# First attention on TensorE: global queries of two pairs in column strips, local probabilities as weights, the result turned back

## The chip, the cores and the metric

The kernel runs on one core of a Trainium2 chip. The metric is device time in microseconds. Before the change three runs took 511.86 to 514.08 us, with a median of 514.04 us. The engines are TensorE (PE, with its weight loads as PEld), VectorE (DVE), ScalarE (ACT), GpSimd (POOL) and SyncE (SP), whose queue issues all DMAs.

## What is computed

Three stages for 4 batches. The first attention has 8 heads of 64, 512 local tokens and 32 global ones. Global queries look at all keys, local queries at the global keys and at a window of 32 to either side. The second stage routes the 576 tokens over 4 experts by a gate (each expert is one causal attention head), and the third is an MLP with a convolution of three taps and a gate.

```python
k_all = np.concatenate([k_g, k_l], axis=2)
out_g = sm(scale * q_g @ k_all.T) @ v_all
mask = np.abs(pos[:, None] - pos[None, :]) <= window
out_l = sm(concat(scale * q_l @ k_g.T, where(mask, scale * q_l @ k_l.T, -1e9))) @ concat(v_g, v_l)
...
a = sm(where(causal, -1e9, scale * q @ k.T))
out += mask * w * (a @ v @ wo[e])
...
h = np.maximum(x @ w_in, 0.0)
gate = 1.0 / (1.0 + np.exp(-conv_out))
return h * gate @ w_out
```

## The kernel before

Every operation is first recorded as a node with a due time (`due`) and an estimated cost (`cost_pe`, `cost_act`, `cost_dve`, `cost_pool`, `cost_dma`). `Recorder.schedule` (lines 227 to 307) then plays the nodes through in estimated time: each engine takes, of the nodes whose inputs and buffers are free, the one with the earliest due time. The order that comes out is written into each engine's queue; on the chip each engine keeps to it. So due times are priorities and not start times, and since `emit` issues everything (line 314), all rows of the trace have that line and are told apart by tile and shape. Due times come from the constants of lines 37 to 40: `PERIOD` between batches, `A_AT` and `A_STEP` for the first attention, `B_AT`, `LAST`, `ITEMS` and `ITEM_STEP` for the second, `C_AT`, `C_HALF` and `C_PROJ` for the MLP, `FOLD` and `WOUT` with their steps for preparing weights.

Heads go in pairs, with the 64 dims of two heads on 128 partitions; a batch has 4 pairs, the run 16. For a pair, `phase_a` (line 670) does this in turn.

- `load_kq` and `load_v` fetch keys and queries in one DMA (tile `raw`, two buffers) and the values in two (`vr`, three buffers for two halves each). The global queries of the pair's two heads are laid out with zeros, so that one matmul over 128 rows gives both heads' scores.
- `scores_g` (571) makes 64 rows of scores (2 heads of 32 queries) over 544 keys in two matmuls of 480 and 64 columns. VectorE takes the maxima, ScalarE the exponentials into `Pg`, VectorE the sums, and POOL scales `Pg`.
- `scores_l` (587) makes the local scores: 16 groups of 32 queries, each over 128 keys, in tiles of 64 rows by 32 columns, after a mask (`lmask`) has been put into PSUM by bf16 matmuls. VectorE takes the maxima, ScalarE eight exponentials into two tiles `Pa`, and POOL scales both by one over the sums (lines 613 and 614).
- `trans_g` and `trans_l` turn `Pg` and `Pa` by transposes on TensorE; ScalarE copies the results out of PSUM (`PGT`, `PA`).
- `pv_l` (637): the values are the weights (128 x 64) and the turned probabilities move, 32 columns each, 32 matmuls a pair. The result has dims on the partitions, as the next stage wants it.
- `pv_end` (650) splits the result into a high and a low part (`xh` by ScalarE, `xl` by VectorE), then does the global queries' values.

In the trace each fp32 matmul that is no transpose stands as two records.

`phase_b` does the second attention: projections of q, k, v from `xh`, `xl`, the gate, then eight items (score, transpose, values). Its turned probabilities lie in `PT` (two buffers) and `PLT`; its results in `oh` and `ol`. `phase_c` does the MLP from `oh` and `ol`, in two halves of eight column blocks with a projection after each.

Weights of the MLP come as 64-bit words. `decode` (437) makes floats of a chunk of 256 columns: four ops on VectorE, an add on POOL, an absolute value on ScalarE and, on VectorE, a guard that zeroes what is too small (line 450). 16 chunks of `w_in` are folded with `wo` on TensorE (`fold_gen`), 16 chunks of `w_out` only split (`wout_gen`). The fold keeps `wo` in the memory of `oh` and `ol`, so the second attention's first results wait for the fold.

PSUM has five buffers `s` (scores and projections) and three buffers `t` (transposes and values).

Of the kernel before, what the change touches and what calls it, by code (L numbers as in the profile page):

```python
# [21 lines left out]
EPS = 1e-9  # L22
# [362 lines left out]
def body(ctx, tc, kq, vA, w_gate, wqk, wv, woT, w_in, conv_w, w_out, cmask, out):  # L385
# [13 lines left out]
    def due(us):  # L399
        rec.due = us  # L400
# [65 lines left out]
    trif = T([128, 4, 4], F32, "trif")  # L466
    cw = T([128, 3, 8], F32, "cw")
# [79 lines left out]
    NPA, NPT = 2, 2  # L547
# [4 lines left out]
    Pg = T([64, 6, 128], F32, "Pg")  # L552
# [3 lines left out]
    QW = SL + 2 * SG  # L556
# [14 lines left out]
    def scores_g(k, q):  # L571

        mg = T([64, 8], F32, "mg", 2)
        gt = PS(5, 96)[:64], PS(64)[:64]
        for z, kk in enumerate((k[:, 32:672].rearrange("p (m c) -> p m c", m=5)[:, :, 32:], k[:, 672:736])):
            if z == 0:
                rec.claim(Pg)
            pe.matmul(gt[z], q[:, SL:], kk, start=True, stop=True)
            dve.tensor_reduce(mg[:, z:z + 1], gt[z], axis=AX.X if z else AX.XY, op=ALU.max, negate=True)
        dve.tensor_scalar(mg[:, 2:3], mg[:, 0:1], mg[:, 1:2], SCALE, op0=ALU.min, op1=ALU.mult)  # L580
        for z, d in enumerate((Pg[:, 0:5, 32:128], Pg[:, 5, 32:96])):
            act.activation(d, gt[z], AF.Exp, bias=mg[:, 2:3], scale=SCALE, accum_out=mg[:, 4 + z:5 + z])
# [4 lines left out]
    def scores_l(k, q):  # L587
# [16 lines left out]
        ml = T([128, 2, 16], F32, "ml", 2)  # L604
        for y in range(2):
            dve.tensor_reduce(ml[:, y, 0:4], t[y], axis=AX.X, op=ALU.max, negate=True)
            dve.tensor_scalar(ml[:, y, 0:4], ml[:, y, 0:4], SCALE, None, op0=ALU.mult)
            for i in range(4):
                act.activation(P[y][:, i], t[y][:, i], AF.Exp, bias=ml[:, y, i:i + 1], scale=SCALE,
                               accum_out=ml[:, y, 4 + i:5 + i])  # L610
        dve.tensor_scalar(ml[:, :, 8:12], ml[:, :, 4:8], EPS, None, op0=ALU.add)
        dve.reciprocal(ml[:, :, 12:16], ml[:, :, 8:12])
        for y in range(2):
            pool.tensor_tensor(P[y], P[y], ml[:, y, 12:16, None].to_broadcast([128, 4, 128]), op=ALU.mult)
        return P

    def trans_g():
        PGT = T([128, 6, 64], F32, "PGT")
        t = PO(6, 64)
        rec.claim(PGT)  # L620
        with rec.group():
            for m in range(6):
                pe.transpose(t[:, m, :], Pg[:, m], ident[:64, :64])
        act.activation(PGT, t, AF.Copy)
        return PGT

    def trans_l(P):
        PA = T([128, 4, 128], F32, "PA", 2)
# [8 lines left out]
    def pv_l(b, c, vr, PA):  # L637

        o = PO(4, 128)
        xh, xl = xs[b, c] = T([128, S], F32R, "xh", XB), T([128, S], F32R, "xl", XB)  # L640
        rec.claim(xh, xl)
        with rec.group():
            for g in range(NG_):
                q = slice(32 * (g % 4), 32 * (g % 4) + 32)
                for y in range(2):
                    pe.matmul(o[64 * y:64 * y + 64, g // 4, q], vr[g // 8][:, g % 8, 64 * y:64 * y + 64], PA[y][:, g // 4, q],
                              start=True, stop=True)
        return o
# [15 lines left out]
    def consts_a():  # L664
        due(-15)
# [26 lines left out]
    def phase_b(b):  # L692
# [265 lines left out]
def host_layout(inputs):  # L958
# [23 lines left out]
    kq = np.zeros((B, H // 2, 2, D, KB + SL + 2 * SG), kl.dtype)  # L982
# [8 lines left out]
    for y in range(2):  # L991
        kq[:, :, y, :, KB + SL + SG * y:KB + SL + SG * y + SG] = pair(inputs["q_g"])[:, :, y]
# [26 lines left out]
```

## Time and profile before

| | |
|---|---|
| Median of 3 runs | 514.04 us (511.86 to 514.08) |
| Profiled execution, its own time | 516.68 us |
| Its span in the trace | 514.9 us |
| TensorE busy | 468.6 us, 91% |
| TensorE weight loads | 400.2 us, 78% |
| VectorE busy | 359.1 us, 70% |
| ScalarE busy | 313.5 us, 61% |
| POOL busy | 155.5 us, 30% |
| Moved by DMA | 44.06 MB |

The profile shows one execution. Busy time is the time in which an engine had an instruction running; matmuls are pipelined and their records overlap, so a busy TensorE need not be at its peak. A wait is put down to the last thing that an engine waited for. What lies outside the span, some 1.8 us here, belongs to the time but not to the trace.

### The profile page before, as it was taken

To read this page: it belongs to the slowest core of one execution; us is meant where nothing else is said; L and a number is where in the kernel's file an instruction comes from. 1 tells how busy PE (TensorE), PEld (TensorE's weight loads), DVE (VectorE), ACT (ScalarE), POOL (GpSimd) and SP (SyncE) were. 2 spreads that over 40 slices of the span, in tenths; PEclk is the share of its full clock that TensorE was granted. 3 is DMA by queue.
4 is the path that set the end of the run, shared out by engine and by line. 5 is a ranking of instruction groups with operands and counts; after the bars stand their busy time and mean duration, and the time that the engine had idled before them with its cause. 6 is when DMAs were issued, how large, how long until landed. Compare 5 with 4: busy or idle time off the path is not lost.

```text
span 514.9 us, 14575 instructions
## 1 busy us (share of the span) xinstructions
PE 468.6 (91%) x5688; PEld 400.2 (78%) x5688; DVE 359.1 (70%) x1026; ACT 313.5 (61%) x1048; POOL 155.5 (30%) x259
## 2 busy tenths in 40 slices
PE   3559869987989799999999999999999999999997
PEld 1346559964678589997779999877888999787896
DVE  1878876898989987385659763667486564665961
ACT  1666564556579776565569864447696764344972
POOL 2335445445771635022440200225212200322000
PEclk9788898998999889999999999999999999999999
DMA  8484533242055060014044030002421000000011
GB/s 308 165 241 163 181 136 104 87 135 95 26 176 178 25 217 22 22 35 127 23 137 134 27 105 1 11 23 68 137 83 66 24 0 3 23 23 1 1 45 45
DMA packets 19045, 44.06 MB, mean 86 GB/s; under 512 B 2848, under 2 KB 8096, under 8 KB 18976
## 3 DMA queue, kind: packets, MB, share of 16 engines
q1 hardware_dynamic: 18976, 43.12, 25.2%
q8 instruction: 45, 0.74, 0.6%
q14 instruction: 24, 0.20, 0.1%
HBM read 38.66 MB, written 4.46 MB: 84 GB/s over the span
## 4 chain that ended last, share of the span: by engine, by line
PE 68%; DVE 16%; DMA 6%; ACT 5%; POOL 3%; issue 2%; SPq 0%; POOLq 0%; ACTq 0%; DVEq 0%
PE s L314 52%; PE t L314 16%; DVE cv L314 7%; DMA raw<-in_kq_dram 3%; DMA w<-in_w_in_dram 2%; DVE hb L314 2%; DVE gl L314 1%; DVE mg L314 1%; DVE stB L314 1%; DVE ml L314 1%; POOL w L314 1%; ACT hb L314 1%; POOL Pa L314 1%; ACT Pa L314 1%; DVE wqkl L314 1%
## 5 line engine op out<-in xcount | busy, mean ns | idle before, releaser
L314 PE MATMUL s<-gh,wuh 128*128 128x272 f32 x256 | 78.9, 308 | 0.4 <-ACT gh L314 0.4
L314 DVE SCALAR_TENSOR_TENSOR cv<-hb,cw,cv 128x272 f32<-128x272 f32 x128 | 66.6, 535 | 16.6 <-ACT cv L314 14.8
L314 POOL TENSOR_SCALAR w<-w,stB,gate 128x128 f32<-128x128 f32 (+3 forms) x64 | 41.5, 659 | 116.0 <-DVE gate L314 51.2
L314 PE MATMUL s<-gl,wuh 128*128 128x272 f32 x256 | 74.9, 293 | 1.4 <-DVE gl L314 1.2
L314 PE MATMUL s<-gh,wul 128*128 128x272 f32 x256 | 74.2, 290 | 0.0
L314 PEld LDWEIGHTS s<-gh,wuh 128*128 128x128 f32 x256 | 48.8, 191 | 5.8 <-issue 3.0
L314 POOL TENSOR_TENSOR Pa<-Pa,ml 128x512 f32<-128x512 f32 x32 | 37.3, 1183 | 46.4 <-DVE ml L314 24.8
L314 PEld LDWEIGHTS s<-gl,wuh 128*128 128x128 f32 x256 | 48.8, 191 | 2.8 <-DVE gl L314 2.6
L314 PE MATMUL s<-raw 64*32 64x128 f32 (+2 forms) x1088 | 43.7, 308 | 7.8 <-DMA raw<-in_kq_dram 6.7
L314 PEld LDWEIGHTS s<-gh,wul 128*128 128x128 f32 x256 | 48.7, 190 | 0.0
L314 ACT ACTIVATE Pa<-s,ml 128x128 f32<-128x128 f32 x128 | 45.3, 378 | 3.3 <-DVE ml L314 2.8
L314 ACT ACTIVATE w<-s,stB 128x128 f32<-128x128 f32 (+3 forms) x64 | 33.4, 527 | 18.8 <-DVE stB L314 10.7
L314 PE MATMUL s<-oh,wfh 128*128 128x274 f32 x128 | 39.8, 311 | 1.1 <-ACT Pa L314 1.1
L314 POOL TENSOR_TENSOR cv<-cv,hb 128x256 f32<-128x256 f32 (+1 forms) x33 | 26.0, 788 | 48.8 <-DVE hb L314 39.3
L314 PEld LDWEIGHTS s<-raw 64*32 64x32 f32 (+1 forms) x1088 | 22.9, 117 | 20.7 <-issue 11.1
L314 DVE COPY PT<-t 128x128 f32<-128x128 f32 (+3 forms) x64 | 29.8, 485 | 12.0 <-PE t L314 11.4
L314 PE MATMUL s<-xh,wqkh 128*128 128x272 f32 x128 | 37.6, 294 | 0.1
L314 PE MATMUL s<-xh,wqkl 128*128 128x272 f32 x128 | 37.4, 292 | 0.0
L314 PE MATMUL s<-xl,wqkh 128*128 128x272 f32 x128 | 37.4, 292 | 0.0
L314 PE MATMUL s<-ol,wfh 128*128 128x274 f32 x128 | 37.3, 291 | 0.0
L314 PE MATMUL s<-oh,wfl 128*128 128x274 f32 x128 | 37.2, 291 | 0.0
L314 DVE TENSOR_REDUCE stB<-s 128x1 f32<-128x128 f32 (+3 forms) x64 | 29.7, 484 | 8.6 <-PE s L314 6.1
(147 smaller groups left out, 1302.8 us busy)
## 6 DMA issues: line engine op xcount, KB each, us to landing
vr<-in_vA_dram SPq DMA_DIRECT2D x32, 512.0 KB, 5.1
raw<-in_kq_dram SPq DMA_DIRECT2D x16, 672.0 KB, 4.7
out_dram<-y SPq DMA_DIRECT2D x32, 136.0 KB, 1.7
w<-in_w_in_dram SPq DMA_DIRECT2D x16, 256.0 KB, 3.5
w<-in_w_out_dram SPq DMA_DIRECT2D x16, 256.0 KB, 2.7
w<-in_wqk_dram SPq DMA_DIRECT2D x4, 256.0 KB, 5.4
w<-in_wv_dram SPq DMA_DIRECT2D x4, 128.0 KB, 4.1
w<-in_woT_dram SPq DMA_DIRECT2D x2, 256.0 KB, 2.7
```

The costliest lines, as they stand in the source:

```text
L314: getattr(n.eng.nc, method)(*map(real, args), **{k: real(v) for k, v in kw.items()})
```

## The change

- `scores_g` takes two pairs at once. Each of the four heads is a matmul of 64 rows by 32 columns with its own column strip, so that 128 rows of scores come out; `Pg` has 128 partitions, and the maxima, exponentials, sums and the scaling are done once for two pairs. The zeros in the global queries' layout are gone.
- Keys and queries come in two DMAs with tiles of their own (`rk`, `rq`, two buffers each).
- `scores_l` no longer scales the probabilities. It returns one over the sums.
- `pv_l`: the turned probabilities (128 x 32) are the weights, the values move with 64 columns. The result has queries on the partitions; VectorE multiplies it by one over the sums into `x`, and `pv_end` turns it back with four transposes. The global values are now `pv_g`.
- `PA`, `PT`, `PLT` (its first 128 keys by four) and `x` share four buffers, `p2`.
- The guard in `decode` goes from one op on VectorE to two on POOL.
- An exponential of one column is done first of all, which loads ScalarE's table.
- `lmask` is due ahead of the first pair's loads.
- All constants of the order are new, and two costs of TensorE.

```diff
-PERIOD, A_AT, A_STEP, LOAD_AHEAD = 60.0, -1.0, 10.0, 20.0
-B_AT, LAST, ITEMS, ITEM_STEP = 30.0, 35.0, 13.5, 2.4
-C_AT, C_HALF, C_PROJ = 75.0, 23.0, 11.0
-FOLD, FOLD_STEP, WOUT, WOUT_STEP = 20.5, 2.5, 75.0, 2.5
+PERIOD, A_AT, A_STEP, LOAD_AHEAD = 54.5, 0.0, 5.0, 21.5
+B_AT, LAST, ITEMS, ITEM_STEP = 29.0, 54.0, 9.0, 2.45
+C_AT, C_HALF, C_PROJ = 80.0, 41.0, 36.5
+FOLD, FOLD_STEP, WOUT, WOUT_STEP = 12.0, 1.45, 75.0, 2.0
...
     if K == 64:
-        return us + 0.052
+        return us + max(0.03, N / 2400 if N > 128 else 0.0)
+    if M == 32 and N == 64:
+        return us + 0.03
...
-        dve.scalar_tensor_tensor(dst, a, GUARD, d, op0=ALU.is_ge, op1=ALU.mult)
+        pool.tensor_scalar(a, a, GUARD, 1.0, op0=ALU.is_ge, op1=ALU.mult)
+        pool.tensor_tensor(dst, a, d, op=ALU.mult)
...
+    due(-30)
+    warm = T([128, 1], F32, "warm")
+    dve.memset(warm, 0.0)
+    act.activation(warm, warm, AF.Exp)
...
-        raw = T([128, KB + QW], F32, "raw", 2)
-        sp.dma_start(raw, kq[n // 4, n % 4])
-        return raw[:, :KB], raw[:, KB:]
+        k, q = T([128, KB], F32, "rk", NRK), T([128, QW], F32, "rq", NRQ)
+        sp.dma_start(k, kq[n // 4, n % 4][:, :KB])
+        sp.dma_start(q, kq[n // 4, n % 4][:, KB:])
+        return k, q
...
+        with rec.group():
+            for z in range(2):
+                for c, (k, q) in enumerate(pairs):
+                    for y in range(2):
+                        kk = k[64 * y:64 * y + 64]
+                        kk = kk[:, 672:736] if z else kk[:, 32:672].rearrange("p (m c) -> p m c", m=5)[:, :, 32:]
+                        r = slice(64 * c + 32 * y, 64 * c + 32 * y + 32)
+                        pe.matmul(gt[z][r] if z else gt[z][r].rearrange("p (m c) -> p m c", m=5),
+                                  q[64 * y:64 * y + 64, SL:], kk, start=True, stop=True)
...
-        for y in range(2):
-            pool.tensor_tensor(P[y], P[y], ml[:, y, 12:16, None].to_broadcast([128, 4, 128]), op=ALU.mult)
-        return P
+        return P, ml[:, 3]
...
-                    pe.matmul(o[64 * y:64 * y + 64, g // 4, q], vr[g // 8][:, g % 8, 64 * y:64 * y + 64], PA[y][:, g // 4, q],
-                              start=True, stop=True)
+                    d = slice(64 * y, 64 * y + 64)
+                    pe.matmul(o[r, i, d], PA[y][:, i, r], vr[g // 8][:, g % 8, d], start=True, stop=True)
+        heads = lambda t: t.rearrange("p i (y d) -> p i y d", d=64)
+        dve.tensor_tensor(heads(x), heads(o), one[:, :, :, None].to_broadcast([128, 4, 2, 64]), op=ALU.mult)
+        return x
...
+            for i in range(4):
+                pe.transpose(t[:, i, :], x[:, i], ident)
...
     def consts_a():
-        due(-15)
+        due(-25)
...
     def phase_a(b):
-        for c in range(4):
+        for c in range(0, 4, 2):
+            at = A_AT + PERIOD * b + A_STEP * c
             n = 4 * b + c
-            at = A_AT + PERIOD * b + A_STEP * c
             due(at - LOAD_AHEAD)
-            kq_ = load_kq(n)
-            vr = load_v(n)
+            kq_ = [load_kq(n), load_kq(n + 1)]
+            vr = []
+            for y in range(2):
+                due(at + A_STEP * y - LOAD_AHEAD)
+                vr.append(load_v(n + y))
             due(at)
-            scores_g(*kq_)
-            due(at + 1)
-            P = scores_l(*kq_)
+            scores_g(kq_)
+            P = []
+            for y in range(2):
+                due(at + 1 + A_STEP * y)
+                P.append(scores_l(*kq_[y]))
             due(at + A_STEP)
             PGT = trans_g()
-            PA = [trans_l(P[y]) for y in range(2)]
-            due(at + A_STEP + 1)
-            o = pv_l(b, c, vr, PA)
-            pv_end(b, c, o, vr, PGT)
+            for y in range(2):
+                due(at + A_STEP * (y + 1))
+                PA = [trans_l(p) for p in P[y][0]]
+                due(at + A_STEP * (y + 1) + 1)
+                x = pv_l(vr[y], PA, P[y][1])
+                pv_end(b, c + y, x)
+                pv_g(b, c + y, vr[y], PGT)
...
-                PT = T([128, 4, 128], F32, "PT", NPT)
+                PT = T([128, 4, 128], F32, "p2", NPT)
```

## Rows read from the trace of the kernel before

**Rows 1.** The page: busy us of each engine, share of the span, instructions.
```profile
PE 468.6 (91%) x5688; PEld 400.2 (78%) x5688; DVE 359.1 (70%) x1026; ACT 313.5 (61%) x1048; POOL 155.5 (30%) x259
```

**Rows 2.** Six stages: length, busy us (instructions), clock (1.00 is 2.4 GHz), DMA share, GB/s.
```profile
0.00:15.00 15.00, 6.18 (x85) 3.61 (x86) 3.54 (x11) 2.63 (x6) 3.29 (x11) 1.00 0.86 311
15.00:75.00 60.00, 44.30 (x761) 31.57 (x759) 49.16 (x118) 37.28 (x142) 29.36 (x31) 0.86 0.52 164
75.00:105.00 30.00, 27.90 (x265) 27.10 (x267) 23.10 (x71) 16.31 (x57) 12.82 (x16) 0.94 0.34 116
105.00:180.00 75.00, 63.82 (x920) 48.66 (x916) 70.12 (x201) 51.59 (x179) 40.57 (x58) 0.95 0.32 107
180.00:450.00 270.00, 267.38 (x3191) 236.83 (x3183) 175.42 (x532) 170.25 (x571) 61.62 (x118) 0.99 0.19 62
450.00:515.00 65.00, 59.07 (x489) 52.42 (x487) 37.71 (x96) 35.39 (x98) 7.87 (x26) 1.00 0.07 23
```

**Rows 3.** Waits of TensorE: line waiting, releaser, us in total, times, longest.
```profile
PE s L314 <- DMA raw<-in_kq_dram: 6.7, 4, 4.8
...
PE t L314 <- POOL Pa L314: 5.4, 6, 3.9
...
PE s L314 <- DVE lmask L314: 4.1, 1, 4.1
...
PE s L314 <- DVE wfl L314: 3.1, 1, 3.1
...
PE t L314 <- DVE PT L314: 1.4, 3, 0.8
```

**Rows 4.** Timeline of the start, all engines: start us, length us, what.
```profile
7.75 1.28 ACT L314 ACT_TABLE_LOAD   x1 [7.75 <-DVE mg L314]
...
10.45 0.40 DVE L314 CAST lmask<-w 128x512 bf16<-128x512 f32 x1
...
22.29 1.12 PE L314 MATMUL t<-ident,Pa 128*128 128x128 f32 x4 [3.85 <-POOL Pa L314]
```

**Rows 5.** Timeline of TensorE alone, 362 to 402 us: the groups of a pair.
```profile
363.82 1.09 PE L314 MATMUL t<-PT,vB 128*64 128x128 f32 x16
...
368.21 0.33 PE L314 MATMUL s<-raw 128*64 128x64 f32 x2
...
368.47 0.58 PE L314 MATMUL t<-ident,Pg 64*128 64x64 f32 x6
...
368.98 1.02 PE L314 MATMUL s<-raw 128*64 128x480 f32 x2
...
373.10 1.03 PE L314 MATMUL t<-ident,Pa 128*128 128x128 f32 x8
...
375.44 1.16 PE L314 MATMUL s<-raw 64*32 64x128 f32 x64
...
377.49 2.06 PE L314 MATMUL t<-PA,vr 128*64 128x32 f32 x64
```

**Rows 6.** Groups by shape: busy us, mean ns of one, idle before them.
```profile
L314 PEld LDWEIGHTS t<-PA,vr 128*64 128x64 f32 x1024 | 31.6, 138 | 2.0 <-issue 0.9 <-ACT hb L314 0.7
...
L314 POOL TENSOR_TENSOR Pa<-Pa,ml 128x512 f32<-128x512 f32 x32 | 37.3, 1183 | 46.4 <-DVE ml L314 24.8 <-DVE ol L314 7.0 <-PE s L314 4.4
...
L314 POOL TENSOR_TENSOR cv<-cv,hb 128x256 f32<-128x256 f32 x32 | 25.8, 805 | 42.1 <-DVE hb L314 32.6 <-ACT Pa L314 4.8 <-DVE ml L314 2.8
...
L314 POOL TENSOR_SCALAR Pg<-Pg,mg 64x768 f32<-64x768 f32 x16 | 16.8, 1050 | 26.2 <-DVE mg L314 21.8 <-PE s L314 4.3 <-ACT PA L314 0.2
...
L314 POOL TENSOR_SCALAR w<-w,stB,gate 128x256 f32<-128x256 f32 x16 | 9.4, 597 | 18.8 <-DVE stB L314 10.5 <-ACT oh L314 4.7 <-PE s L314 3.3
...
L314 DVE SCALAR_TENSOR_TENSOR cv<-hb,cv 128x256 f32<-128x256 f32 x32 | 17.0, 534 | 2.8 <-ACT hb L314 2.8
...
L314 DVE TENSOR_TENSOR xl<-t,xh 128x512 fp32r<-128x512 f32 x16 | 11.0, 686 | 7.0 <-ACT xh L314 6.9
```

More of the change, by code (lines that the diff above doesn't have):

```diff
@@ L546, in body @@
     XB = 4
-    NPA, NPT = 2, 2
+    NPA, NPT = 2, 4
+    NRK, NRQ, NXQ = 2, 2, 1
     xs = {}
     lmask = T([128, 512], BF, "lmask")
-    Pg = T([64, 6, 128], F32, "Pg")
+    Pg = T([128, 6, 128], F32, "Pg")
     due(-5)
@@ L569, in load_v, with scores_g @@
         return vr
[L571 to L579, printed above, removed]
+    def scores_g(pairs):
+        mg = T([128, 8], F32, "mg", 2)
+        gt = PS(480), PS(64)
+        rec.claim(Pg)
+        with rec.group():
[7 more added lines that the diff above has]
+                                  q[64 * y:64 * y + 64, SL:], kk, start=True, stop=True)
+        for z in range(2):
+            dve.tensor_reduce(mg[:, z:z + 1], gt[z], axis=AX.X, op=ALU.max, negate=True)
         dve.tensor_scalar(mg[:, 2:3], mg[:, 0:1], mg[:, 1:2], SCALE, op0=ALU.min, op1=ALU.mult)
         for z, d in enumerate((Pg[:, 0:5, 32:128], Pg[:, 5, 32:96])):
-            act.activation(d, gt[z], AF.Exp, bias=mg[:, 2:3], scale=SCALE, accum_out=mg[:, 4 + z:5 + z])
+            act.activation(d, gt[z] if z else gt[z].rearrange("p (m c) -> p m c", m=5), AF.Exp, bias=mg[:, 2:3],
+                           scale=SCALE, accum_out=mg[:, 4 + z:5 + z])
         dve.tensor_scalar(mg[:, 6:7], mg[:, 4:5], mg[:, 5:6], EPS, op0=ALU.add, op1=ALU.add)
@@ L603, in scores_l @@
                                   k[rows[y], 32 * FIRST[g]:32 * FIRST[g] + 128], start=False, stop=(i == 3))
-        ml = T([128, 2, 16], F32, "ml", 2)
+        ml = T([128, 4, 4, 2], F32, "ml", 3)
         for y in range(2):
-            dve.tensor_reduce(ml[:, y, 0:4], t[y], axis=AX.X, op=ALU.max, negate=True)
-            dve.tensor_scalar(ml[:, y, 0:4], ml[:, y, 0:4], SCALE, None, op0=ALU.mult)
+            dve.tensor_reduce(ml[:, 0, :, y], t[y], axis=AX.X, op=ALU.max, negate=True)
+            dve.tensor_scalar(ml[:, 0, :, y], ml[:, 0, :, y], SCALE, None, op0=ALU.mult)
             for i in range(4):
[L609 to L612, printed above, removed]
-        for y in range(2):
-            pool.tensor_tensor(P[y], P[y], ml[:, y, 12:16, None].to_broadcast([128, 4, 128]), op=ALU.mult)
-        return P
-    def trans_g():
[L618 to L624, printed above, removed]
+                act.activation(P[y][:, i], t[y][:, i], AF.Exp, bias=ml[:, 0, i, y:y + 1], scale=SCALE,
+                               accum_out=ml[:, 1, i, y:y + 1])
+        dve.tensor_scalar(ml[:, 2], ml[:, 1], EPS, None, op0=ALU.add)
+        dve.reciprocal(ml[:, 3], ml[:, 2])
+        return P, ml[:, 3]
+    def trans_g():
+        PGT = T([128, 6, 128], F32, "PGT")
+        for z in range(2):
+            t = PO(3, 128)
+            rec.claim(PGT[:, 3 * z:3 * z + 3])
+            with rec.group():
+                for m in range(3):
+                    pe.transpose(t[:, m, :], Pg[:, 3 * z + m], ident)
+            act.activation(PGT[:, 3 * z:3 * z + 3], t, AF.Copy)
         return PGT
     def trans_l(P):
-        PA = T([128, 4, 128], F32, "PA", 2)
+        PA = T([128, 4, 128], F32, "p2", NPT)
         t = PO(4, 128)
@@ L635, in trans_l, with pv_l, pv_end, pv_g @@
         return PA
-    def pv_l(b, c, vr, PA):
+    def pv_l(vr, PA, one):
         o = PO(4, 128)
+        x = T([128, 4, 128], F32, "p2", NPT)
+        rec.claim(x)
+        with rec.group():
+            for g in range(NG_):
+                i, r = g // 4, slice(32 * (g % 4), 32 * (g % 4) + 32)
+                for y in range(2):
[4 more added lines that the diff above has]
+        return x
+    def pv_end(b, c, x):
         xh, xl = xs[b, c] = T([128, S], F32R, "xh", XB), T([128, S], F32R, "xl", XB)
+        t = PO(4, 128)
         rec.claim(xh, xl)
         with rec.group():
-            for g in range(NG_):
-                q = slice(32 * (g % 4), 32 * (g % 4) + 32)
-                for y in range(2):
-                    pe.matmul(o[64 * y:64 * y + 64, g // 4, q], vr[g // 8][:, g % 8, 64 * y:64 * y + 64], PA[y][:, g // 4, q],
-                              start=True, stop=True)
-        return o
-    def pv_end(b, c, o, vr, PGT):
+            for i in range(4):
+                pe.transpose(t[:, i, :], x[:, i], ident)
+        d = slice(32, 544)
+        act.activation(xh[:, d], t.rearrange("p i q -> p (i q)"), AF.Copy)
+        sub(xl[:, d], t.rearrange("p i q -> p (i q)"), xh[:, d])
+    def pv_g(b, c, vr, PGT):
         xh, xl = xs[b, c]
-        x = slice(32, 544)
-        act.activation(xh[:, x], o.rearrange("p i q -> p (i q)"), AF.Copy)
-        sub(xl[:, x], o.rearrange("p i q -> p (i q)"), xh[:, x])
         o = PO(512)
@@ L786, in phase_b @@
             scale_pool(PL[z], PL[z], ms[:, 7:8])
-        PLT = T([128, 5, 128], F32, "PLT")
+        PLT, PLE = T([128, 4, 128], F32, "p2", NPT), T([32, 128], F32, "PLE")
         t = PO(4, 128)
-        rec.claim(PLT)
+        rec.claim(PLT, PLE)
         with rec.group():
@@ L862, in pv_last @@
                             pe.matmul(o[64 * y:64 * y + 64, p, :32], vB[:kr, j, 64 * e:64 * e + 64],
-                                      PLT[:kr, j, 32 * e:32 * e + 32], start=(j == 0), stop=(j == 4))
+                                      (PLT[:, j] if j < 4 else PLE)[:, 32 * e:32 * e + 32], start=(j == 0), stop=(j == 4))
             act.activation(oh[:, :, 512:544], o[:, :, :32], AF.Copy)
@@ L990, in host_layout @@
     kq[..., KB:KB + SL] = pair(inputs["q_l"])
-    for y in range(2):
-        kq[:, :, y, :, KB + SL + SG * y:KB + SL + SG * y + SG] = pair(inputs["q_g"])[:, :, y]
+    kq[..., KB + SL:] = pair(inputs["q_g"])
     return dict(
```

12 lines of the change are left out of this document (7 added, 5 removed).

## The prediction

> **What bounds the kernel now.** I read the page's busy times first, then the table by stages, the waits of the matmul engine, the timeline of the start, the timeline of one attention pair in mid-run, and last the groups by shape. TensorE is busy for 468.6 of 514.9 us [rows 1], and the stages say where the rest lies [rows 2]. From 180 to 450 us TensorE is busy 267.4 of 270 us: there each microsecond of matmul work that goes away is a microsecond gained, and no other engine bounds. From 0 to 75 us it idles for 75 - 50.5 = 24.5 us, from 75 to 180 for 13.3, from 450 on for some 6. In the first 15 us the DMA engines are 86% busy, so the loads bound; from 15 to 75 us nobody is full (TensorE 74%, VectorE 82%, DMA 52%) and the granted clock is 0.86, that is, part of it runs at 1.2 GHz: a chain of waits. From 105 to 180 us VectorE is 93% busy and TensorE waits for it. The named waits of TensorE [rows 3]: 6.7 us for q and k to land, 5.4 for the scaling of the probabilities on POOL, 4.1 for the mask, 3.1 for the fold of the weights. The start itself [rows 4]: the table load of ScalarE stands on the chain at 7.75 us, the mask is cast at 10.45 only, behind the global softmax on VectorE, and the first transpose of local probabilities comes at 22.29.
>
> **Matmul work per pair.** Rows 5 give one pair at full clock; lengths there overlap their neighbours by some 0.07 us, on both sides of each difference.
> - Global scores: 1.02 + 0.33 = 1.35 us a pair. Now two pairs go as four 32-column strips, twice the records for two pairs. The local scores show that strips run together: 64 records of 128 columns in 1.16 us are 18 ns each, where 16 records of 128 columns on two strips (PT into vB) take 1.09 us, 68 ns each. So I take 1.35 us for two pairs: -0.68 a pair. Bounds: nothing better than -0.68, since the columns still have to stream once; if the strips go in turn, four times 1.35 for two pairs, +1.35 a pair. I take the first, as the row of local scores is the nearest (same 64 rows by 32 columns).
> - Global transposes: six of 64 rows now (0.58), then six of 128 rows for two pairs. A transpose of Pa is 1.03 / 8 = 0.13 us, so 0.77 / 2 = 0.39: -0.19 a pair.
> - Local values: 64 records in 2.06 us, 32 ns each. Swapped, a record streams 64 columns on one of four strips. From 68 ns for 128 columns on two strips: 68 x 64/128 x 2/4 = 17 ns, like the 18 ns of the local scores: 64 x 17 = 1.1 us, -0.96 a pair. Bounds: -0.96, and +2.3 with strips in turn (64 x 68 = 4.35).
> - Four more transposes to turn the result back: +0.52.
>
> Sum: -0.68 - 0.19 - 0.96 + 0.52 = -1.31 us a pair. Of 16 pairs the first batch's four lie where TensorE idles, and I give them nothing. Twelve pairs: **-15.7 us**.
>
> **The start.** The local probabilities are no longer scaled before their transposes; the scale goes onto the result. So the 5.4 us for POOL go (almost all of it early). The mask is loaded ahead of the first pair and so is no longer behind the softmax: the 4.1 us go, and the first local scores need only the first pair. The fold gets earlier due times (12 + 1.45 a step for 20.5 + 2.5): the wait of 3.1 us for it goes. The table load leaves the chain, but the loads of the first 7 us cover most of it: nothing counted. Against that, the global scores now wait for two pairs' q and k: 672 KB more at the 311 GB/s of the first stage are 2.2 us. The extra DMA issue a pair (k and q apart) lands in SP's queue, which mostly sits waiting for buffers; nothing, unless a load waits there behind one whose buffer is late. Together -12.6 + 2.2: **-10.4 us**; bounds 0 (the DMAs set the pace anyway) and -20 (most of the 24.5 us).
>
> **VectorE and POOL.** The guard of the decoded weights leaves VectorE: 32 x 0.53 = 17.0 us. The global reductions and small steps halve. The scaling of the result comes: a 128x512 op on PSUM, by the subtraction xl 0.69 us, 16 x 0.69 = 11 us. VectorE's sum falls by more than 10 us, mostly before 180 us. TensorE idles 11.2 us from 105 to 180; I take a third of that: **-4 us** (0 to -9). POOL loses 37.3 us of scaling and half of 16.8, and gets 32 x (0.60 + 0.81) = 45 us for the guard [rows 6]: even, in total at 30% of the span. But a decoded chunk's way gets 0.60 + 0.81 - 0.53 = 0.9 us longer; the two chunks in flight cover it, and if they don't, 16 fold chunks cost up to 14 us of the start (in its bounds). ScalarE's global exponentials halve too; it is not the bound.
>
> **The added wait.** TensorE must now wait between the values and the transposes back, for VectorE's multiply. Behind it in TensorE's queue stand the transposes, and behind them whatever the plan put next; ScalarE's and VectorE's copies of x and the projections wait for that. Nothing below zero is possible here; above, a full trip is VectorE's queue plus 0.69 us. The nearest row is the same kind of trip already there: TensorE waits for VectorE's copies PT 1.4 us in 64 times [rows 3]. The plan puts other work in between. I take 0.2 us a pair: **+3.2 us**.
>
> Sum: -15.7 - 10.4 - 4 + 3.2 = -26.9. The profiled execution took 516.68 us, so 489.8; the median of the runs, 514.04, stands 2.6 us below it, so **487 us** is forecast for the median. Differences under 0.5%, 2.6 us, count as no change.
>
> The due times of everything else move too (the period, the projections of the MLP much later). From 180 to 450 us that can gain nothing much, since 2.6 us is all the idle time there; at the end some 3 us may be had if the batch before leaves matmuls to fill in.
>
> **Rivals.**
> - Half of it: either the start stays bound by the DMAs (no gain there), or waits eat the matmuls saved. Without the start's term 498 us, without the pairs' 503: about 500 us, range 494 to 510. For it: DMA is at 52% from 15 to 75 us, and two pairs in one go need their buffers at once. Chance 0.20.
> - No change: PA, PT, PLT and the new x share four buffers, where PT and PA had two each and PLT its own. If that makes the second attention and the next first attention wait for each other, the saved 27 us are stood idle: 514. Against it: before 180 us only is there little else to do for TensorE. Chance 0.06.
> - Slower, by the trip over VectorE: TensorE stands at each of the 16 transposes back for the multiply, 0.69 us, one 128x512 op ahead of it, 0.69, and two ops of a decode, 0.6 each: 2.6 us, in place of my 0.2, +38 us, 525 us. It decides from 26.9 / 16 + 0.2 = 1.9 us a pair. For it: VectorE is 93% busy from 105 to 180 us. Against it: from 180 us on it is 65% busy, and PT shows no such wait. Chance 0.08.
> - Slower, by strips in turn: +1.35 and +2.3 us a pair for the two terms above, 12 x (1.35 + 2.3 + 0.33) = +48 in place of -15.7, 551 us. Against it: the weight loads of the local values now last 138 ns and come every 32 ns, on all 128 rows [rows 5, 6], so loads and matmuls of such records do overlap. Chance 0.04. The Trainium skill ("TensorE: Matmul & The Clock Gate", What overlaps and what doesn't) says that a weight load overlaps with matmuls in flight only when its row group differs; by that the swapped values, which use all the rows, would go one after another. The trace disagrees for the form before the change, at 32 ns a record.
>
> **How the numbers follow.** Forecast 0.62, with 474 to 498 for itself: down to 474 with -20 at the start and -7 more from VectorE and the end, up to 498 where the start gives nothing back and the pairs nearly all. The range over the cases is 474 to 508: above it lie no change and the two slower cases, 0.18. Faster by over 0.5%: 0.62 + 0.20 = 0.82; within 0.06; slower 0.08 + 0.04 = 0.12.
>
> **What would show it.** Right: in a mid-run pair 16 records of global scores in about 1.4 us for two pairs, local values in about 1.1 us, TensorE's busy time some 15 to 20 us less; the first transposes of Pa before 15 us; idle time to 75 us near 14 us; no line of TensorE waiting for x above a few us. Wrong: records of the values at 30 ns or more; a wait of TensorE for VectorE's x of over 1.9 us a pair; the fold's matmuls waiting for POOL's guard in place of the wait of 3.1 us; or TensorE idle between 180 and 450 us where it is full now.

## The result, and the profile after

The changed kernel takes 473.6 us (median of 4 runs, 470.36 to 478.98) against 514.06 us. The ratio is 0.920, with a 95% interval of 0.9145 to 0.9258. So it is faster by 40 us. The run of 478.98 us is a slow one, at a mean clock of 0.975 for 0.989 to 0.993 in the other three, and the ratio leaves it out. The forecast was 487 us with a range of 474 to 508, so the sign was right and the time lies just under the range. The profiled execution took 474.14 us with a span of 472.3; the profiled one of before had a span of 514.9. The spans differ by 42.6 us, and the sum forecast 26.9.

The page of the changed kernel, busy time of each engine [rows 1]:

```profile
PE 440.8 (93%) x5768; PEld 382.9 (81%) x5768; DVE 338.6 (72%) x970; ACT 305.8 (65%) x1017; POOL 168.9 (36%) x285
```

TensorE is busy for 27.8 us less and idle for 14.8 us less (31.5 for 46.3). The stages, columns as in [rows 2]:

```profile
0.00:15.00 15.00, 7.80 (x100) 5.12 (x101) 4.49 (x16) 6.67 (x25) 3.28 (x11) 1.00 0.90 306
15.00:75.00 60.00, 51.80 (x898) 41.94 (x897) 43.48 (x120) 40.11 (x145) 38.54 (x48) 0.94 0.58 196
75.00:105.00 30.00, 27.38 (x449) 21.59 (x456) 26.19 (x85) 18.38 (x66) 24.01 (x32) 1.00 0.37 125
105.00:180.00 75.00, 70.44 (x1052) 59.88 (x1033) 66.68 (x193) 52.22 (x183) 48.00 (x68) 0.98 0.37 120
180.00:450.00 270.00, 264.71 (x3152) 236.28 (x3151) 189.03 (x538) 178.00 (x575) 54.96 (x127) 1.00 0.15 51
450.00:473.00 23.00, 18.71 (x145) 18.07 (x143) 8.77 (x21) 10.38 (x27) 0.10 (x1) 0.99 0.10 37
```

Idle time from 15 to 75 us is 8.2 us (15.7 before), from 105 to 180 us 4.6 (11.2), and from 180 to 450 us 5.3 (2.6): the middle got slightly worse. The granted clock of the second stage went from 0.86 to 0.94. The waits of TensorE [rows 3]:

```profile
PE t L314 <- POOL Pg L314: 3.9, 3, 2.3
PE s L314 <- DVE lmask L314: 3.7, 1, 3.7
PE s L314 <- POOL gl L314: 2.9, 6, 0.9
...
PE t L314 <- DVE p L314: 1.1, 2, 0.8
```

The wait for POOL's scaling of `Pa` is gone, and one for `Pg` is the costliest now. A wait for the mask still stands, but at the very start, where TensorE has nothing else to do yet: the mask is cast at 3.25 us and no longer at 10.45. `p` are all four-buffer tiles (PA, PT, PLT, x) together. `gl` is the fold's: its 2.9 us stand where 3.1 us of waiting for `wfl` stood before. The start [rows 4]:

```profile
0.71 1.28 ACT L314 ACT_TABLE_LOAD   x1 [0.71 <-PEq L1046]
...
3.25 0.43 DVE L314 CAST lmask<-w 128x512 bf16<-128x512 f32 x1 [0.59 <-DMA w<-in_cmask_dram]
...
9.64 1.36 PE L314 MATMUL t<-ident,Pa 128*128 128x128 f32 x4
...
21.26 0.66 PE L314 MATMUL t<-ident,p 128*128 128x128 f32 x4 [0.81 <-DVE p L314]
```

The first transposes of `Pa` come at 9.64 us and no longer at 22.29. In mid-run, TensorE alone [rows 5]:

```profile
180.35 1.12 PE L314 MATMUL s<-rk,rq 64*32 64x480 f32 x16
...
198.88 1.17 PE L314 MATMUL t<-vr,p 128*32 128x64 f32 x64
...
202.21 0.60 PE L314 MATMUL t<-ident,p 128*128 128x128 f32 x4
```

Two pairs' global scores (16 records, both widths) take 1.12 us, the local values 1.17 us a pair, the transposes back 0.60. The guard's two ops on POOL [rows 6]:

```profile
L314 POOL TENSOR_SCALAR hb<-hb 128x256 f32<-128x256 f32 x32 | 35.9, 1120 | 11.1 <-ACT hb L314 11.0
...
L314 POOL TENSOR_TENSOR cv<-hb,cv 128x256 f32<-128x256 f32 x32 | 24.5, 767 | 2.3
```

**The account.** Each span is busy plus idle time. In windows of 2.5 us, the busy time multiplied by one minus the granted clock is what running at 1.2 GHz added to it: 12.1 us before, 4.9 us now. That leaves

| us | before | after | difference |
|---|---|---|---|
| TensorE busy, without what the lower clock adds | 456.5 | 435.9 | -20.6 |
| added by stretches at 1.2 GHz (30.6 us of them before, 10.3 after) | 12.1 | 4.9 | -7.2 |
| TensorE idle | 46.3 | 31.5 | -14.8 |
| span | 514.9 | 472.3 | -42.6 |

Call these work, clock and idle time. They are read off one execution each, and the split of busy time by the clock is rough: experiments 2 to 6, 11 and 12 have the TensorE operations of the changed kernel and read 432.4 to 441.0 us of work, and experiment 1, with the operations of before, reads 450.1 us for 456.5. So a difference of some 6 us in work says nothing by itself. The same three are given for the experiments. The theories: **W**, the work and the waits that the new operations take away are the gain; **O**, the new order is a large part of it; **C**, the clock is; **N**, any plan but the fitted one loses about the same, whatever was edited.

### The profile page after: what moved, and what is told of

It is laid out like the page before. It is cut to its first block, busy times and chain, and to the rows that moved or that the text cites. A ratio compares the mean times of both kernels' runs of the same rounds, so it can differ in the third digit from the quotient of the medians.

```text
span 472.3 us, 14650 instructions
## 1 busy us (share of the span) xinstructions
PE 440.8 (93%) x5768; PEld 382.9 (81%) x5768; DVE 338.6 (72%) x970; ACT 305.8 (65%) x1017; POOL 168.9 (36%) x285
## 4 chain that ended last, share of the span: by engine, by line
PE 59%; DVE 16%; POOL 9%; ACT 6%; issue 5%; DMA 3%; SPq 0%; DVEq 0%; POOLq 0%; ACTq 0%
PE s L314 43%; PE t L314 16%; DVE cv L314 6%; POOL cv L314 4%; POOL hb L314 3%; DVE hb L314 2%; DVE gl L314 2%; DVE stB L314 2%; DVE ml L314 2%; ACT cv L314 2%; DMA vr<-in_vA_dram 1%; ACT hb L314 1%; DMA w<-in_w_gate_dram 1%; POOL gl L314 1%; DMA rq<-in_kq_dram 1%
## 5 line engine op out<-in xcount | busy, mean ns | idle before, releaser
L314 POOL TENSOR_SCALAR w<-w,stB,gate 128x128 f32<-128x128 f32 (+3 forms) x64 | 42.9, 681 | 91.5 <-DVE glast L314 44.2
L314 DVE SCALAR_TENSOR_TENSOR cv<-hb,cw,cv 128x272 f32<-128x272 f32 x128 | 64.4, 515 | 15.1 <-ACT cv L314 12.4
L314 POOL TENSOR_SCALAR hb<-hb 128x256 f32<-128x256 f32 (+1 forms) x33 | 36.7, 1112 | 11.1 <-ACT hb L314 11.0
L314 PE MATMUL s<-oh,wfh 128*128 128x274 f32 x128 | 38.2, 299 | 1.2 <-DVE kl L314 0.8
L314 DVE COPY p<-t 128x128 f32<-128x128 f32 (+3 forms) x64 | 29.9, 484 | 10.9 <-PE t L314 10.8
L314 ACT ACTIVATE cv<-cv 128x272 f32<-128x272 f32 x64 | 27.4, 429 | 13.5 <-DVE cv L314 12.7
L314 PE MATMUL t<-ident,w 128*128 128x128 f32 x176 | 30.3, 282 | 5.1 <-POOL w L314 2.7
```

The lines of the kernel that those rows point to most:

```text
L314: getattr(n.eng.nc, method)(*map(real, args), **{k: real(v) for k, v in kw.items()})
```

## The experiments

Every edit makes the recorder plan anew, unless said otherwise.

**1. The new order alone, on the kernel before.**

```diff
 (before)
-PERIOD, A_AT, A_STEP, LOAD_AHEAD = 60.0, -1.0, 10.0, 20.0
+PERIOD, A_AT, A_STEP, LOAD_AHEAD = 54.5, 0.0, 5.0, 21.5
...
+FOLD, FOLD_STEP, WOUT, WOUT_STEP = 12.0, 1.45, 75.0, 2.0
```

> The kernel before with the new constants of the order alone (its operations and costs as before). Theory W (the gain is TensorE work that is gone, and waits that the new operations remove): nearly no gain, 505 to 520 us, TensorE busy within 4 us of 468.6. Rival O (the new order alone fills the idle time of the first 180 us and the end): 500 us or less, busy time unchanged but idle time down by 14 us or more. Rival C (the clock: TensorE spends less time at 1.2 GHz): busy time falls below 463 with the same work.

511.6 us, ratio 0.996 (0.993 to 1.000). Idle time fell by 6.4 us, but the stretches at 1.2 GHz grew to 44.4 us and gave 7.5 back; the work reads 6.4 us less for the same operations. Alone, the order is worth at most 4 us, and W's expectation held.

**2. The old order, on the changed kernel.**

```diff
 (after)
-PERIOD, A_AT, A_STEP, LOAD_AHEAD = 54.5, 0.0, 5.0, 21.5
+PERIOD, A_AT, A_STEP, LOAD_AHEAD = 60.0, -1.0, 10.0, 20.0
...
+FOLD, FOLD_STEP, WOUT, WOUT_STEP = 20.5, 2.5, 75.0, 2.5
```

> The changed kernel with the constants of the order from before. Theory W: 474 to 484 us, since the work stays gone. Rival O: 490 us or more, with idle time of TensorE near 46 us as before the change.

496.7 us, ratio 0.969 (0.962 to 0.976), 23 us slower than with its own order. Idle time is 44.0 us, as O said, and clock 10.6. Its stages up to 180 us, columns as in [rows 2]; its waits of TensorE for tiles `p` in all; and the transposes back by themselves (busy us, mean ns, idle before them):

```profile
0.00:15.00 15.00, 7.81 (x101) 5.51 (x102) 4.81 (x16) 6.87 (x25) 3.27 (x11) 0.91 0.89 301
15.00:75.00 60.00, 51.10 (x893) 42.06 (x891) 44.49 (x120) 40.69 (x146) 38.19 (x47) 0.91 0.58 196
75.00:105.00 30.00, 27.15 (x302) 22.60 (x301) 24.93 (x87) 14.13 (x48) 25.34 (x34) 0.94 0.29 95
105.00:180.00 75.00, 64.03 (x906) 52.66 (x905) 63.18 (x163) 52.32 (x173) 50.06 (x69) 0.98 0.36 114
```

```profile
PE t L314 <- DVE p L314: 6.3, 8, 2.5
```

```profile
L314 PE MATMUL t<-ident,p 128*128 128x128 f32 x64 | 10.1, 280 | 4.8 <-DVE p L314 4.5
```

Here is the added wait of the prediction: of 6.3 us for tiles `p`, 4.5 stand before the transposes back, where the fitted order has 0.8 (its row is shown in experiment 8). Idle time before 75 us is 16.1 us (24.5 in the kernel before), from 105 to 180 us 11.0 (11.2), and after 180 us 14.0 (8.5). So the operations under the old order take 8.4 us of idle time off the start, nothing off the stage where VectorE was to give way, and put 5.5 us on the rest. By the spans they bring 20.0 us (work 16.2, idle time 2.3, clock 1.5), and the new order on top of them 22.6 (idle time 12.5, clock 5.7, and 4.4 that read as work). By the medians the operations alone are worth 17 us, the order alone 2, and both together 40. The two new costs of TensorE in the plan stayed in this run.

**3. The MLP's constants of before alone.**

```diff
 (after)
-C_AT, C_HALF, C_PROJ = 80.0, 41.0, 36.5
+C_AT, C_HALF, C_PROJ = 75.0, 23.0, 11.0
```

> The changed kernel with the MLP's constants of before (C_AT, C_HALF, C_PROJ) alone. Theory O (the order fitted to the new operations is worth some 20 us, and the MLP put off until it can fill TensorE's idle time is the most of it): 485 us or more, with TensorE idle over 10 us between 105 us and the end more than the 13.5 us of the changed kernel. Rival N (any move of the plan away from the fitted one costs about the same, whichever constant it is): as far from 473.6 as the run with PERIOD alone changed. Rival W (work only): 474 to 478 us.

500.5 us, ratio 0.970 (0.963 to 0.977). This one line loses as much as the whole old order. Its stages, columns as in [rows 2]:

```profile
105.00:180.00 75.00, 69.14 (x967) 58.15 (x965) 66.47 (x174) 52.71 (x181) 51.35 (x71) 0.98 0.34 110
180.00:420.00 240.00, 228.61 (x2917) 199.95 (x2917) 155.21 (x471) 149.10 (x496) 47.55 (x100) 1.00 0.18 58
420.00:494.00 74.00, 68.06 (x549) 60.63 (x548) 45.55 (x118) 42.16 (x116) 8.33 (x28) 1.00 0.07 24
```

From 180 to 420 us TensorE is idle for 11.4 us; in the changed kernel it is busy 235.65 of those 240 us, so idle for 4.35. Of the 22.2 us in span, 11.1 are idle time, 6.0 clock and 5.1 read as work. O holds, with the MLP's line as its main part, and N does not: one line costs 27 us, a unit of PERIOD 12 or less. How the line does it is not shown. That an MLP done early leaves less to put between the steps of the two attentions fits the trace, but it is not isolated by it: by 300 us this run has done 434 of the MLP's matmul records (on `wfh`, `wfl`, `wuh` and `wul`) for 372 in the changed kernel, and between 300 and 420 us it has 338 for 431, with 4.5 us of idle time there for 0.6; but 3 us more idle time stand before 300 us too.

**4. The weights' constants of before alone.**

```diff
 (after)
-FOLD, FOLD_STEP, WOUT, WOUT_STEP = 12.0, 1.45, 75.0, 2.0
+FOLD, FOLD_STEP, WOUT, WOUT_STEP = 20.5, 2.5, 75.0, 2.5
```

> The changed kernel with FOLD, FOLD_STEP, WOUT, WOUT_STEP of before. Theory O with the MLP as the most of it: 474 to 482 us. If the earlier fold is what opens the first 100 us: 485 us or more, the fold's last matmul over 15 us later, idle time before 105 us up by over 5 us. Rival N: as the run with PERIOD alone changed.

476.5 us, ratio 0.926 (0.918 to 0.934), not to be told from 0.920. The fold's last matmul starts at 103.6 us for 96.4, and idle time moves between stages (5.7 us for 2.6 from 75 to 105 us, 1.7 for 4.4 from 180 to 420 us), 2.3 us more in all. A term of its own for the early fold can't be told from nothing here.

**5 and 6. PERIOD one unit up and one down.**

```diff
 (after)
-PERIOD, A_AT, A_STEP, LOAD_AHEAD = 54.5, 0.0, 5.0, 21.5
+PERIOD, A_AT, A_STEP, LOAD_AHEAD = 55.5, 0.0, 5.0, 21.5
```

> The changed kernel with PERIOD 55.5 for 54.5, all else the same: the measure of what a small move of the plan costs. Rival N: 10 us or more slower than the changed kernel. Otherwise within 4 us of 473.6, and the distances of the other runs are those of their edits.

485.3 us, ratio 0.9405 (0.933 to 0.948). Of the 11.2 us in span, 6.7 are clock, 3.4 idle time, 1.1 work.

> The changed kernel with PERIOD 53.5 for 54.5. Rival N (each plan has its own clock and waits, so that a unit of PERIOD to either side costs some 10 us): 480 to 492 us, work at full clock within 2 us of the changed kernel's 435.9, the rest clock and idle time. Theory O (PERIOD has a direction): 474 us or less.

478.4 us, ratio 0.930 (0.925 to 0.935); its interval overlaps that of the changed kernel. N holds on one side only: a unit of PERIOD up costs 12 us, a unit down nothing that is sure.

**7. The local values as before.**

```diff
 (after)
+        for y in range(2):
+            pool.tensor_tensor(P[y], P[y], ml[:, 3, :, y, None].to_broadcast([128, 4, 128]), op=ALU.mult)
...
-                    pe.matmul(o[r, i, d], PA[y][:, i, r], vr[g // 8][:, g % 8, d], start=True, stop=True)
+                    pe.matmul(o[64 * y:64 * y + 64, g // 4, q], vr[g // 8][:, g % 8, 64 * y:64 * y + 64], PA[y][:, g // 4, q],
+                              start=True, stop=True)
...
-            for i in range(4):
-                pe.transpose(t[:, i, :], x[:, i], ident)
```

> The changed kernel with the local values as before: POOL scales the probabilities, the values are the weights, no transposes back. By my terms 0.44 us of TensorE work a pair (16 pairs, 7 us) and the start's waits for POOL (up to 5.4 us) come back: 480 to 488 us. If the swap is worth nothing because the transposes back eat it: 474 to 478 us with TensorE busy within 3 us. If the chain through POOL was what mattered: busy within 3 us, but 484 us or more by idle time before 75 us.

504.5 us, ratio 0.982 (0.974 to 0.991), 31 us slower. All three expectations missed. Work is up by 5.3 us, near the 7 that the prediction priced but no more than the split's error; idle time is up by 10.9 and the clock by 14.6 (44.4 us at 1.2 GHz).

**8. The global queries as before.**

```diff
 (after)
-            scores_g(kq_)
+                scores_g(*kq_[y])
...
-                        pe.matmul(gt[z][r] if z else gt[z][r].rearrange("p (m c) -> p m c", m=5),
-                                  q[64 * y:64 * y + 64, SL:], kk, start=True, stop=True)
+            pe.matmul(gt[z], q[:, SL:], kk, start=True, stop=True)
```

> The changed kernel with the global queries as before: one pair at a time, zeros in the layout, 64 rows of scores. By my terms 0.87 us of TensorE work a pair comes back, 14 us, of which 10 to 14 show: 484 to 489 us, busy time of TensorE up by 11 to 15 us. Rival: the strips save work only where TensorE idles anyway: under 479 us. Rival: the doubled VectorE and ScalarE steps of the softmax delay the start as well: over 492 us with idle time before 75 us up by over 5 us.

504.9 us, ratio 0.983 (0.976 to 0.990), again 31 us. Work is up by 11.6 us (priced at 14), the clock by 12.7, idle time by 7.3, of that 1.5 from 15 to 75 us. All three expectations missed here too. The groups of this run and of the run with the old values, then of the changed kernel, then of the kernel before (busy us, mean ns):

```profile
L314 PE MATMUL s<-rk,rq 128*64 128x480 f32 x32 | 19.6, 701 | 6.0 <-DMA rq<-in_kq_dram 6.0
...
L314 PE MATMUL s<-rk,rq 128*64 128x64 f32 x32 | 5.2, 247 | 0.0
```

```profile
L314 PE MATMUL t<-p,vr 128*64 128x32 f32 x1024 | 33.3, 224 | 0.0
```

```profile
L314 PE MATMUL t<-vr,p 128*32 128x64 f32 x1024 | 18.9, 222 | 0.0
...
L314 PE MATMUL t<-ident,p 128*128 128x128 f32 x64 | 10.0, 279 | 1.5 <-DVE p L314 0.8 <-DVE ol L314 0.6
L314 PE MATMUL s<-rk,rq 64*32 64x480 f32 x64 | 9.8, 682 | 0.0
...
L314 PE MATMUL s<-rk,rq 64*32 64x64 f32 x64 | 2.7, 240 | 0.0
```

```profile
L314 PE MATMUL t<-PA,vr 128*64 128x32 f32 x1024 | 33.1, 223 | 0.0
...
L314 PE MATMUL s<-raw 128*64 128x480 f32 x32 | 18.4, 660 | 5.7 <-DMA raw<-in_kq_dram 4.8 <-DVE xl L314 1.0
...
L314 PE MATMUL s<-raw 128*64 128x64 f32 x32 | 5.5, 258 | 2.0 <-DMA raw<-in_kq_dram 1.9
```

The scores went from 19.6 + 5.2 to 9.8 + 2.7 us, the values from 33.3 to 18.9, and the transposes back cost 10.0. Against the kernel before, scores, values and transposes back together went from 57.0 to 41.4 us; with the global transposes (9.7 to 8.8) the operations' own rows are 16.5 us less.

Two halves of one change, each worth 31 us of 40 when taken out: they can't be added. Of each 31 us, 20 or more are clock and idle time. That they come from constants fitted to other operations is likely by experiments 2, 3 and 5, but argued: no constants were fitted to either of these two kernels.

**9. The clock in the start.** The kernel before, order unchanged, with idle matmuls in two gaps.

```diff
 (before)
         with rec.group():
+            fill(t, n)
             for i in range(4):
...
+            fill(o, 12 if (b, c) == (0, 1) else 0)
             for m, g in enumerate(PGW):
```

> The kernel before, order of the work unchanged, with 21 matmuls whose results nobody reads (128x512 bf16, written into PSUM that is overwritten next) in two gaps of TensorE at 18 and 33 us, so that it does not idle there. They are added work. Theory C (the stretches at 1.2 GHz follow those gaps, and cost time): the granted clock between 17 and 45 us rises to 0.95 or more, TensorE's own work in it gets shorter, and the time falls by 2 to 6 us, to 508 to 512. Rival (the clock is a companion of the waits and costs nothing, as the waits set the pace there): the clock rises, the time stays within 2 us of 514 or rises. Second rival: the clock does not follow the gaps and stays low.

514.2 us, ratio 0.999 (0.996 to 1.003). Two stretches, first before, then with the matmuls filled in:

```profile
17.00:27.00 10.00, 4.79 (x85) 2.88 (x82) 9.45 (x26) 6.55 (x21) 6.29 (x6) 0.66 0.37 112
35.00:45.00 10.00, 6.92 (x131) 4.97 (x132) 8.56 (x19) 3.72 (x10) 6.37 (x7) 0.66 0.33 119
```

```profile
17.00:27.00 10.00, 6.27 (x130) 4.01 (x133) 9.44 (x25) 6.73 (x21) 6.43 (x6) 1.00 0.43 114
35.00:45.00 10.00, 10.00 (x194) 7.21 (x193) 8.95 (x20) 4.31 (x14) 6.87 (x7) 0.94 0.49 166
```

In both stretches 0.66 became 1.00 and 0.94. But the matmuls shorten the gaps and don't close them (1.7 us of waiting for `Pa` are left of 3.9), and the stage as a whole gained little clock, 0.86 to 0.89, as it now runs at 1.2 GHz for some 10 us from 60 to 71 us, where the kernel before has 3.4:

```profile
15.00:75.00 60.00, 48.72 (x784) 33.44 (x785) 50.36 (x124) 37.70 (x146) 29.88 (x31) 0.89 0.56 173
```

The time didn't move by what can be measured, as the rival had it. That the waits set the pace in the start fits this; with so little clock gained in all, the run doesn't exclude that a clock at 2.4 GHz throughout would be worth something there.

**10. The clock where TensorE is full.** The kernel of experiment 5 with such matmuls in four late gaps.

```diff
 (after, PERIOD 55.5)
+                fill(whole, 5 if z and b == 2 else 0)
...
+            fill(t.rearrange("p i q -> p (i q)"), 3 if (b, c) == (3, 2) else 0)
...
+                fill(o.rearrange("p a b -> p (a b)"), (0, 0, 4, 3)[b])
```

> The kernel with PERIOD 55.5, order unchanged, with 15 matmuls whose results nobody reads (128x512 bf16) in its four short gaps at 305, 348, 350 and 432 us, ahead of its three late stretches at 1.2 GHz, where TensorE is full. They are 3.3 us of added work, most of it in idle time. Theory C (the clock is worth its time where TensorE is the bound): the clock stays up there, the 6 to 7 us that those stretches cost go, and the time falls from 485.3 by 3 to 7 us, to 478 to 482. Rival: the clock falls anyway, and the time rises by up to 2 us.

483.0 us, ratio 0.941 (0.937 to 0.945), against 0.9405 without. Three stretches of the kernel of experiment 5, then with the matmuls:

```profile
300.00:315.00 15.00, 13.50 (x95) 11.91 (x91) 11.59 (x30) 12.13 (x40) 3.08 (x9) 0.89 0.09 34
350.00:360.00 10.00, 9.94 (x153) 9.22 (x154) 3.13 (x10) 5.72 (x19) 0.10 (x1) 0.66 0.02 9
430.00:440.00 10.00, 8.95 (x85) 8.29 (x84) 1.11 (x3) 3.43 (x10) 1.08 (x6) 0.83 0.09 30
```

```profile
300.00:315.00 15.00, 13.45 (x162) 10.44 (x156) 10.54 (x28) 10.49 (x37) 4.28 (x10) 1.00 0.18 56
350.00:360.00 10.00, 8.14 (x172) 6.04 (x155) 3.61 (x10) 4.66 (x21) 0.00 (x0) 1.00 0.17 57
430.00:440.00 10.00, 9.49 (x99) 8.60 (x99) 1.93 (x9) 4.20 (x13) 1.07 (x6) 1.00 0.09 30
```

The clock stayed at 1.00 in all three, and indeed from 106 us to within 1 us of the end; the same work comes some 4 us later in this run. The matmuls did not fill the gaps, though. The timeline of TensorE shows that most ran right behind them:

```profile
352.73 0.81 PE L314 MATMUL t<-lmask,identb 128*128 128x512 bf16 x2 [0.57 <-DVE p L314]
...
354.88 1.02 PE L314 MATMUL t<-lmask,identb 128*128 128x512 bf16 x4 [0.91 <-ACT PLE L314]
```

The gaps of 0.57 and 0.91 us are those of experiment 5 (0.58 and 0.91), and 0.98 us stand for 1.15 at the first place; only the last, 0.58 us, is taken up. The matmuls are work themselves (3.6 us more in the account), and the profiled execution fell to 1.2 GHz in another place, at 97 us. C isn't confirmed as a gain that can be had this way. How clock and time go together is seen better within one kernel: the four runs of experiment 5 have one order and one program, and the three with a mean clock of 0.972 to 0.978 took 485.3 to 485.4 us, the one with 0.989 took 479.4. It is one run, and it doesn't say what raised its clock.

**11. The guard back on VectorE.**

```diff
 (after)
-        pool.tensor_scalar(a, a, GUARD, 1.0, op0=ALU.is_ge, op1=ALU.mult)
-        pool.tensor_tensor(dst, a, d, op=ALU.mult)
+        dve.scalar_tensor_tensor(dst, a, GUARD, d, op0=ALU.is_ge, op1=ALU.mult)
```

> The changed kernel with the guard of the decoded weights back on VectorE (one op for two on POOL). By my terms VectorE gets 17 us more work, and TensorE idles up to 4 us more between 105 and 180 us: 476 to 480 us. If POOL's longer chain cost the fold time: 473 or less, with POOL's waits for TensorE (gl) gone. Rival N: 480 to 490 us, as any other plan.

483.5 us, ratio 0.9385 (0.933 to 0.944). Idle time is 31.8 us, the same as in the changed kernel; the 10 us lie in the clock (18.0 us for 4.9, with 3.5 less read as work). The time is N's, 480 to 490. TensorE's waits for POOL's `gl` are down to 1.2 us from 2.9. VectorE's busy time is 341.8 us for 338.6, only 3.2 more though it does the guard. Groups of VectorE in this run, then in the changed kernel:

```profile
L314 DVE SCALAR_TENSOR_TENSOR hb<-w,hb 128x256 f32<-128x256 uint32 x32 | 14.3, 447 | 0.1
L314 DVE SCALAR_TENSOR_TENSOR cv<-hb,cv 128x256 f32<-128x256 f32 x32 | 14.0, 440 | 1.6 <-ACT hb L314 1.2
...
L314 DVE TENSOR_SCALAR hb<-w 128x256 int32<-128x256 int32 x32 | 10.6, 334 | 3.7 <-DMA w<-in_w_in_dram 2.2 <-DMA w<-in_w_out_dram 1.6
```

```profile
L314 DVE SCALAR_TENSOR_TENSOR hb<-w,hb 128x256 f32<-128x256 uint32 x32 | 16.7, 522 | 0.2
...
L314 DVE TENSOR_SCALAR hb<-w 128x256 int32<-128x256 int32 x32 | 13.7, 431 | 4.8 <-DMA w<-in_w_in_dram 2.9 <-POOL cv L314 1.2 <-DMA w<-in_w_out_dram 0.6
```

The guard costs 14.0 us, but the two other ops shown got 5.5 us cheaper with 58 us less of POOL's work beside them (110.7 for 168.9), and a small one, `ml<-ml` of 128x4, another 4.1 (9.7 to 5.6). The Trainium skill ("SBUF — State Buffer", on the shared port pair) says that a VectorE op in a two-port mode and a GpSimd op block each other for a whole instruction, and that one with two SBUF inputs does so against a GpSimd op that reads SBUF. The means fit that (522 for 447 ns, 431 for 334), and the medians hardly differ (426 for 419, 316 for 290), so the loss sits in some of the 32 instances; which of them waited for POOL is not shown.

**12. Without the early table load, and the mask later.**

```diff
 (after)
-    act.activation(warm, warm, AF.Exp)
...
-        due(-25)
+        due(-15)
```

> The changed kernel without the early table load and with the mask due at -15 as before. By my terms the wait for the mask comes back and the table load stands on the chain again: 475 to 480 us, with the first local scores 4 to 7 us later. If the loads cover it: 473 to 475 us. Rival N: 480 to 490 us.

481.4 us, ratio 0.936 (0.931 to 0.940). Its first stage:

```profile
0.00:15.00 15.00, 3.83 (x16) 0.85 (x16) 2.30 (x9) 2.33 (x5) 3.33 (x11) 1.00 0.87 288
```

TensorE is busy 3.83 us there and not 7.80, so 4.0 us of idle time come back. But they are not the prediction's wait of 4.1 us for the mask, which doesn't stand in this run's waits at all. TensorE waits for `rq` (6.9 us) and for `Pg`:

```profile
PE t L314 <- POOL Pg L314: 6.1, 2, 5.0
```

The table load stands on the chain at 11.07 us, the mask is cast at 13.78, behind the global softmax, and the first transposes of `Pa` come at 21.55 us and not at 9.64. Both edits are in this run, and it can't tell them apart. The time is N's again, 480 to 490.

No experiment gave a version faster than the changed kernel. The four shared buffers, the keys and queries in two DMAs and the plan's two new costs were not tried alone.

## Why the prediction was right or wrong

The direction was right and the work was priced in the right size; what failed is the term for the new order, which was put at nothing. The sum was 15.7 us short of the spans' difference (42.6 for 26.9). By its steps:

- **"The due times of everything else move too ... can gain nothing much"** is the step that failed. It looked at the idle time of the kernel before, 2.6 us from 180 to 450 us, and not at what the new operations make of it under the old order: experiment 2 has 44.0 us idle in all, 14.0 of them after 180 us for 8.5 before. The new order is worth 22.6 us of span (23 of the medians) to the new operations, and 2 us to the old ones (experiment 1). Without the fitted order the kernel stands at 496.7 us, without the MLP's line at 500.5.
- **The work per pair** was priced at -1.31 us, -15.7 for twelve pairs. A pair in mid-run shows -1.17: global scores from 1.35 us to 1.12 for two pairs, global transposes from 0.58 to 0.99 for two pairs, values from 2.06 to 1.17, transposes back 0.60 for the 0.52 priced. The rows of the whole kernel give -16.5 us for all 16 pairs, and the account with the same order on both sides -16.2 (experiment 2 against the kernel before) and -14.2 (the changed kernel against experiment 1). So 4 to 6 us of the table's -20.6 are not the operations'. The rival of strips in turn fell: records of the values come every 18 ns, so what the Trainium skill says of weight loads ("TensorE: Matmul & The Clock Gate", What overlaps and what doesn't) does not hold for this shape either.
- **"The first batch's four lie where TensorE idles, and I give them nothing"** is not settled. TensorE is busy 51.8 of 60 us from 15 to 75 us, for 44.3 before, so that stage has less room to hide work; but the readings above differ by as much as the four pairs are worth.
- **The clock** was named as a symptom and left out of the sum: -7.2 us, -1.5 of them under the old order already. This term failed by omission. In experiments 9 and 10 the clock stayed up where idle matmuls were put into or behind gaps; they don't show that lifting it pays by itself.
- **The start**, -10.4, and **VectorE**, -4, came out in size together: idle time before 180 us fell by 15.2 (37.8 to 22.6), and before 75 us it is 15.4 us for the 14 expected. That was luck in part: under the old order it fell by 7.9, all of it before 75 us, and the rest came with the new order. Of the split, the mask's 4.1 is not shown by itself, as experiment 12 moves the table load too, to which the sum gave nothing. The earlier fold's 3.1 can't be told from nothing (experiment 4), and 2.9 us of waiting for POOL's `gl` took its place, one of the prediction's signs of being wrong. VectorE's relief was next to nothing (experiment 11: idle time equal). POOL's guard costs 60.4 us (35.9 + 24.5) for the 45 priced: the compare takes 1.12 us for the 0.60 of its nearest row.
- **The added wait** of +3.2 us was 4.5 under the old order and is 0.8 under the new one. Even 4.5 is 0.28 us a pair, far from the 2.6 of the slower rival.

So the forecast of 487 lay between the operations alone (497) and the operations with an order fitted to them (474). That it came as near as 13 us is luck in part: it took too much for the operations' waits and nothing for the order. Its lower end, 474, comes out only with the 7 us for VectorE and the end in place of the 4 in the sum (487 - 9.6 - 3); as 7 us more, as it is worded, it would be 470. Why a small move of the plan costs up to 12 us is told by the account (clock and idle time), but not why these constants and not their neighbours; that stays open.

## What to carry to other kernels

Price the work that goes and the idle time that goes apart, and check the work by the rows of the operations themselves: a split of busy time by the clock read the same operations up to 9 us apart here. When a change comes with a new order, ask what idle time the new operations would have under the old one, not what the old kernel had. And where a planner fits an order to costs, taking one part out may price that part plus a misfit: here two halves cost 31 us each of a whole of 40.

## What the runs showed of the hardware that was not expected

A compare and multiply of 128x256 on POOL takes 1.12 us where a multiply by two scalars takes 0.60 [rows 6]. Most of it does not go with the length: the one such op of 128x24 in the changed kernel took 0.84 us, a product of two tiles of that size 0.24. VectorE's decode ops got 75 and 97 ns cheaper on the mean, 7 and 26 ns in the median, when POOL had the guard taken off it. TensorE's clock fell to 1.2 GHz within a stretch in which it was busy throughout (350 to 360 us of experiment 5: 9.94 of 10 us), after gaps of 0.6 and 0.9 us before and between short transposes and value matmuls at 348 to 350 us. In experiment 10 the same gaps were there, with idle matmuls of 128x512 right behind them, and the clock stayed at 2.4 GHz; that is one execution of each. Column strips of 32 over 64 or 128 rows ran beside each other for fp32 at 18 ns a record.
